# Half-width seven-product blocks in groups 1 to 3 of the last up projection of an fp32 SwiGLU layer

## The chip, the cores and the metric

The kernel runs on one core of a Trainium2 chip. The metric is device time in microseconds of one execution, the median of the runs shown. The core has a matrix engine (TensorE, PE in the profile, with its weight loads apart as PEld), VectorE (DVE), ScalarE (ACT), GpSimd (POOL) and SyncE (SP), which issues most of the DMA transfers. The engines run side by side, each through its own list of instructions in order; semaphores make one wait for another. TensorE takes one operand as weights, loaded beforehand, streams the other past them, and leaves its results in PSUM banks, from which ScalarE and VectorE read. All other on-chip data lie in SBUF.

## The reference

Attention over 8 batches of 12 heads with 448 tokens and 64 dimensions, with q and k normalised, and then a SwiGLU layer with 768 inputs and outputs and 1536 hidden columns over the 3584 tokens. All is fp32.

```python
q_n, k_n = rmsnorm(q, g_q), rmsnorm(k, g_k)
attn = softmax(q_n @ k_n.transpose(0, 1, 3, 2) / sqrt(64)) @ v
x = attn.transpose(0, 2, 1, 3).reshape(3584, 768)
g = x @ w_gate
val = x @ w_val
out = (g * sigmoid(g) * val) @ w_out
```

## The kernel before, in words

The function `fast` does everything for inputs of the usual size. Attention goes in pairs of heads. The layer goes in four blocks of two batches (`block`, n = 0 to 3), each with an **up** phase (gate and value products, silu, their product) and a **down** phase (output). Attention for the next block is laid into a block's time; the last block has none beside it.

The products are not plain matrix products. The input of a block is cut into 3 by 2 blocks, and the weights into 3 by 3, and a scheme with 15 instead of 18 block products is used: sums of weight blocks ("sides", made once and kept in DRAM as `up_sides` and `down_sides`) multiply sums of input blocks (`xs`, made per block), and each result is added into one or more of six sums. `UP_ORDER` is the order of the 15 products x, `UP_SUMS` the order in which the sides lie in DRAM, and `UP_READ` says into which sum (t0, t1, d, t3, t4, t5) a product goes, how, and which of six results k it completes. `FRESH` products open a PSUM bank, others add to one.

The up phase has four groups g of output columns. `up_product` (L1453) does one product for one group, once for gate (which = 0, PSUM tiles `mm`) and once for value (which = 1, tile `at`). Each is two matmuls of 128 by 128 weights with 448 tokens (L1474), a matmul of fp32 runs as two passes. One reader then takes the bank: ScalarE for a copy (L1409), VectorE for an addition or a subtraction (L1411, L1413, L1415). Gate sums lie in `gt`, value sums in `v0` to `v5`. When a result is complete, ScalarE's silu writes to a PSUM tile `st` (L1551) and VectorE multiplies it by the value sum into `gt` (`weigh`, L1554). `up_load` (L1569) brings the sides of five products at a time.

After a group, `combine` makes parts of the down phase's inputs: `hs` half 0 from results 0 and 1 (product 6, L1185) and half 1 from result 4 (product 1, L1189), for each group; product 10 then needs one long combine over all groups. `down_product` (L1663) does 15 products with four matmuls (one for each group) for two halves of the output, and begins with product 6, whose matmuls stream `hs` half 0, group by group.

The order of the instructions is not written by hand. `Order` (L365) collects pieces of work, each with an engine, a length, a due time `when`, a `rank` that brings it forward, and the pieces it must follow. `run` then places piece after piece on its engine as the planned times allow. Reads of PSUM banks have rank 60, silu and `weigh` rank 0, so reads come first.

Of the kernel before, what the change touches and what calls it, by code (L numbers as in the profile page):

```python
# [9 lines left out]
F32 = mybir.dt.float32  # L10
# [483 lines left out]
def fast(  # L494
# [73 lines left out]
        rr=4, ws=2, **{x + str(i): 1 for x in "vw" for i in range(6)},  # L568
# [14 lines left out]
    OFTEN = dict(w1=0, w2=1, w3=2, w4=3, rows=4)  # L583
# [52 lines left out]
    WS = 10 * NC2 * P  # L636
    up_sides = [dram.tile([P, 2, NC2, 15, P], F32, name=f"up_sides{g}") for g in range(NG)]
    down_sides = dram.tile([P, 2, NG, 15, P], F32, name="down_sides")

# [26 lines left out]
    UP, DOWN, BOTH = 30 * NG * PRODUCT, 90.7, 170.0  # L666
# [3 lines left out]

    def block_start(n):
        return FIRST + n * (UP + BOTH) + MORE * (n > 0)

    def block_end(n):
        return block_start(n) + UP + MORE * (n == 0)
# [722 lines left out]
    }  # L1398
    DOWN_READ = {
# [17 lines left out]
    def load_sides(key, sides, part, sums):  # L1417

        n = 2 * (NC2 if sums is UP_SUMS else NG)
        to = take(*key, [P, WS])[:, 0 : n * len(part) * P]  # L1420
# [18 lines left out]
    def block(n):  # L1439
        add = order.add  # L1440
        start = block_start(n)
        unit = (block_end(n) - start) / (30 * NG)
# [10 lines left out]
        def up_product(g, step, x, which, load, key):  # L1453
            nonlocal last
            when = start + (2 * (15 * g + step) + which) * unit

            b = ("BCDAE".index(CHAIN[x]) % 2 if CHAIN[x] != "E" else 0) ^ (g % 2) ^ (n > 0)
# [111 lines left out]
        def up_load(g, piece):  # L1569
            key = ("ws", (n, g, piece))  # L1570
            load = add(
                "SP", 1.2, start + (30 * g + 10 * piece) * unit - 24.0,
# [7 lines left out]

        for g in range(NG):
            steps = [(step, which) for step in range(15) for which in range(2)]
            if n == 0 and g == 0:
                steps[: 2 * HEAD] = sorted(steps[: 2 * HEAD], key=lambda of: of[::-1])
            for step, which in steps:
                if step % 5 == 0 and which == 0:
                    key, load = up_load(g, step // 5)
                up_product(g, step, UP_ORDER[step], which, load, key)
        up_done[n] = last
        if n < NB - 1:  # L1590
# [3 lines left out]
            )  # L1594
        bank_read[:] = [free[0, 0], free[0, 1]]
# [32 lines left out]
        for g in range(NG):  # L1628
            when = start + 30 * (g + 1) * unit + 1.0
# [3 lines left out]
        combine(10, h1, b1, None, block_end(n) + 3.0, [*all_hidden, *made[1], up_done[n]])  # L1633
# [5 lines left out]
        def down_product(step, x, s):  # L1639
# [3 lines left out]
            key = ("ws", (n, "o", piece))  # L1643
            size = 2 if piece < 7 else 1
            if piece not in loads:
# [3 lines left out]
                    after=[*last_load, *(weights["down", i] for i in range(2 * NG))], takes=[key],  # L1649
# [8 lines left out]
            def emit():  # L1658
# [3 lines left out]
                for g in range(NG):  # L1662
                    nc.tensor.matmul(  # L1663
                        banks[s][:, 0:S], w[:, s, g, at], where[x][:, g],
# [198 lines left out]
```

## Time and profile before

| what | before |
|---|---|
| time, median of 3 runs | 1455.13 us (1453.11 to 1456.28) |
| span of the profiled execution | 1452.0 us |
| last block, up phase, group 0 | 1174 to 1219 us |
| last block, up phase, groups 1 to 3 | 1219 to 1354 us |
| last block, down phase | 1354 to 1446 us |
| up phase of block 1 | about 473 to 654 us |

The profile shows one execution on the core, in microseconds from the start of the span. The span is what the profiler saw of that execution, from its first to its last instruction; the execution has no other time of its own on record beside the runs in the first row. In a row of the profile a group of instructions stands as line, engine, operation, tile written from tiles read, shapes and count, then the busy time and the mean of one in ns, then the idle time of the engine ahead of it and what ended that. A row of the timeline begins with start and length; on PE a row with x4 is four passes that follow one another, and its length includes the time until the last is out. In a row of windows each engine has its busy time and its count; then come the granted clock, the share of the DMA engines and GB/s.

### The profile page before, as it was taken

Reading aid. Unit: us, or ns where it says so; the run is one execution under the profiler, and the core shown is the slowest. Engines: PE = TensorE matmul, PEld = TensorE weight load, DVE = VectorE, ACT = ScalarE, POOL = GpSimd, SP = SyncE. Lnnn points to the kernel's source line nnn. Section 1 sums busy time; section 2 is a strip of 40 time slices with the busy share of each in tenths; the row PEclk is TensorE's granted clock in tenths of the full one; section 3 lists DMA queues with packets and bytes.
Section 4 is the critical chain, followed back from the end, with each engine's and each line's share of the span. In section 5 each row is a group of like instructions: output and inputs, shape, how many; then the busy total and the mean of one; then the engine's idle time right before and its main releaser. Section 6 shows DMA issues by size and latency. Waiting matters only on the chain.

```text
span 1452.0 us, 19362 instructions
## 1 busy us (share of the span) xinstructions
PE 1426.0 (98%) x6736; PEld 689.5 (47%) x6736; DVE 879.8 (61%) x1485; ACT 601.6 (41%) x1210; POOL 405.7 (28%) x476
## 2 busy tenths in 40 slices
PE   8999999999999999999999999999999999999997
PEld 4455454534444455544444455544444445555553
DVE  5889876878866434546877642455686644442533
ACT  6875444476653222356564122345555322212100
POOL 4756666625443000022443200011434300000000
PEclk9999999999999999999999999999999999999999
DMA  7778979854643533433644623443463452322235
GB/s 196 217 219 268 352 266 310 260 149 90 129 103 64 133 102 92 114 113 70 122 98 86 138 74 107 107 112 93 85 126 77 95 135 73 108 73 90 69 100 110
DMA packets 410416, 193.29 MB, mean 133 GB/s; under 512 B 280004, under 2 KB 390852, under 8 KB 410308
## 3 DMA queue, kind: packets, MB, share of 16 engines
q1 hardware_dynamic: 399040, 190.57, 49.1%
q10 hardware_dynamic: 11140, 1.38, 0.7%
q8 instruction: 55, 0.90, 0.3%
q14 instruction: 53, 0.43, 0.1%
q0 software_dynamic: 128, 0.00, 0.0%
HBM read 157.29 MB, written 34.60 MB: 132 GB/s over the span
## 4 chain that ended last, share of the span: by engine, by line
PE 90%; DMA 3%; DVE 2%; ACT 2%; SPq 1%; issue 1%; POOL 1%; ACTq 0%; DVEq 0%; POOLq 0%
PE at L1474 25%; PE mm L1474 25%; PE mm L1663 23%; PE at L1049 8%; PE st L970 7%; PE st L1080 1%; PE mm L1080 1%; DMA out_dram<-spare 1%; SPq L768 1%; DMA work<-in_k_dram 1%; ACT es L985 1%; DMA xs<-in_moe_w_gate_dram 0%; PE st L908 0%; DMA v<-in_v_dram 0%; ACT work L918 0%
## 5 line engine op out<-in xcount | busy, mean ns | idle before, releaser
L1474 PE MATMUL at<-xs,ws 128*128 128x448 f32 x960 | 401.2, 540 | 2.5 <-DVE v L1413 1.4
L1474 PE MATMUL mm<-xs,ws 128*128 128x448 f32 x960 | 401.7, 541 | 0.2 <-DVE hs L1315 0.2
L1474 PEld LDWEIGHTS at<-xs,ws 128*128 128x128 f32 x960 | 181.4, 190 | 184.7 <-issue 166.7
L1474 PEld LDWEIGHTS mm<-xs,ws 128*128 128x128 f32 x960 | 182.2, 190 | 180.7 <-issue 177.9
L888 POOL TENSOR_TENSOR work<-work,rr 128x448 f32<-128x448 f32 x72 | 71.8, 1016 | 467.5 <-DVE rr L715 341.6
L1663 PE MATMUL mm<-gt,ws 128*128 128x448 f32 x448 | 175.5, 543 | 0.0
L970 PE MATMUL st<-work 64*64 64x448 f32 (+1 forms) x1536 | 151.2, 501 | 10.3 <-ACT work L918 4.9
L985 ACT ACTIVATE es<-st 128x896 f32<-128x896 f32 x129 | 114.2, 914 | 101.6 <-PE at L1049 87.8
L1411 DVE TENSOR_TENSOR gt<-gt,mm 128x448 f32<-128x448 f32 x64 | 39.7, 621 | 188.1 <-PE mm L1474 161.7
L1663 PE MATMUL mm<-hs,ws 128*128 128x448 f32 x384 | 151.3, 544 | 0.0
L990 POOL TENSOR_TENSOR sums<-es 128x896 f32<-128x896 f32 x36 | 77.2, 2145 | 176.8 <-PE st L1080 83.7
L1663 PEld LDWEIGHTS mm<-gt,ws 128*128 128x128 f32 x448 | 83.6, 190 | 83.0 <-issue 80.8
L1551 ACT ACTIVATE st<-gt 128x448 f32<-128x448 f32 x96 | 52.3, 547 | 159.1 <-DVE gt L1415 85.7
L1409 ACT COPY gt<-mm 128x448 f32<-128x448 f32 x80 | 42.6, 532 | 157.5 <-PE mm L1474 157.4
L1049 PE MATMUL at<-es,v 64*64 64x448 f32 (+1 forms) x1032 | 106.0, 507 | 0.0
L1663 PEld LDWEIGHTS mm<-hs,ws 128*128 128x128 f32 x384 | 71.3, 190 | 71.0 <-issue 70.1
L970 PEld LDWEIGHTS st<-work 64*64 64x64 f32 x1536 | 50.9, 133 | 79.1 <-issue 37.4
L1409 ACT COPY v<-at 128x448 f32<-128x448 f32 x96 | 51.0, 532 | 80.4 <-PE at L1474 79.6
L990 POOL TENSOR_TENSOR sums<-sums,es 128x896 f32<-128x896 f32 x36 | 76.0, 2112 | 2.8
L1049 PEld LDWEIGHTS at<-es,v 64*64 64x64 f32 (+1 forms) x1032 | 44.1, 134 | 56.2 <-issue 50.4
L1554 DVE SCALAR_TENSOR_TENSOR gt<-st,v 128x448 f32<-128x448 f32 x96 | 59.7, 622 | 7.3 <-DVE v L1415 0.5
L1411 DVE TENSOR_TENSOR v<-v,at 128x448 f32<-128x448 f32 x64 | 39.8, 621 | 39.6 <-PE at L1474 39.5
(170 smaller groups left out, 1550.5 us busy)
## 6 DMA issues: line engine op xcount, KB each, us to landing
ws<-up_sides SPq DMA_DIRECT2D x32, 1024.0 KB, 5.6
ws<-down_sides SPq DMA_DIRECT2D x16, 1024.0 KB, 5.7
ws<-down_sides SPq DMA_DIRECT2D x28, 512.0 KB, 4.8
ws<-up_sides SPq DMA_DIRECT2D x16, 768.0 KB, 4.9
out_dram<-spare SPq DMA_DIRECT2D x168, 56.0 KB, 2.1
v<-in_v_dram SPq DMA_DIRECT2D x96, 96.0 KB, 2.5
ws<-up_sides SPq DMA_DIRECT2D x32, 256.0 KB, 5.9
ws<-up_sides SPq DMA_DIRECT2D x16, 512.0 KB, 5.8
```

Source lines behind the costliest of these rows:

```text
L888: nc.gpsimd.tensor_tensor(out=tiles["t", m][:, x], in0=tiles["qk", (m, x)], in1=rr.to_broadcast([P, NC, C]), op=ALU.mult,)
L970: nc.tensor.matmul(st[ds(D * x, D), h, 0:n], tiles["KT", m][rows, ds(P * j + D * of_keys, D)], tiles["QT", m][rows, ds(Q * of_queries, n)] ...
L985: nc.scalar.activation(e, tiles["st", (m, j)][:, :, 0 : S * width(j) // P], AF.Exp)
L990: nc.gpsimd.tensor_tensor(out=to, in0=tiles["e", (m, 0)] if j == 1 else to, in1=e, op=ALU.add)
L1049: nc.tensor.matmul(tiles["at", (m, x)][ds(D * h, D), ds(0, Q) if early else queries], tiles["v", m][rows, j, h], tiles["e", (m, j)][rows, ...
L1080: nc.tensor.matmul(to[ds(D * h + C * x, C)], halves[:, x] if half else many[:, 0:C], term[:, h, 0:Q] if half else term[:, h, ts(x, Q)], st ...
L1409: nc.scalar.copy(to, ps)
L1411: nc.vector.tensor_tensor(out=to, in0=old, in1=ps, op=ALU.add)
L1474: nc.tensor.matmul(ps(), w[:, which, c, at], xs[:, SLOT[x], c], start=fresh and c == 0, stop=c == NC2 - 1, skip_group_check=True,)
L1551: nc.scalar.activation(take(*act, [P, 2, TB])[:, 0, 0:S], to, AF.Silu)
L1554: nc.vector.scalar_tensor_tensor(to, tiles[act][:, 0, 0:S], 1.0 / SCALE, tiles[ready], op0=ALU.mult, op1=ALU.mult,)
L1663: nc.tensor.matmul(banks[s][:, 0:S], w[:, s, g, at], where[x][:, g], start=fresh and g == 0, stop=g == NG - 1, skip_group_check=True,)
```

## The change

In the last block, groups 1 to 3 (`SEVEN = {3: (1, 2, 3)}`) do each product x in another way. A product is two weight chunks (inputs) times gate and value (outputs) times two halves of 224 tokens, which is a 2 by 2 by 2 block product: eight half-width matmuls. A scheme of the Strassen-Winograd kind does it with seven, which are spread over four streams with PSUM banks of their own:

- X: A11 and S2 into an `mm` bank; Y: S1 and S3 into an `at` bank; Z: A12 and A22 into an `st` tile; W: S4 into half a bank of a second `st` tile. A11 to A22 are the chunk and token quarters of `xs`; S1 to S4 are sums and differences of them.
- Z and W run two products behind X and Y (`LAG`).
- Each stream is read and summed as the results were before, at 448 columns for X, Y and Z and 224 for W. When a result is complete in all four streams, POOL adds X's and Y's parts in four half-width additions (`plus`) and Z to the gate (`sow`, 448 wide), VectorE adds W's part to the value (`top`, 224 wide, both inputs in SBUF), ScalarE's silu goes from `gt` into free columns of the two W banks, and VectorE multiplies as before.
- Sums t5 and t0 have a second place for every second group (`sums`, `v`); the place of t4's Y sum is one.
- `halves_of` makes S1 to S4 for all 15 products on POOL during group 0 (60 subtractions and additions of 224 columns).
- The seven weight combinations are made ahead by `prepare`: 15 units for POOL (four subtractions of 384 columns each) with their loads and a store to DRAM (`up7`), 8 of them in the up phase of block 1 and 7 in that of block 2, planned 16 us apart. The last block loads three products at a time, X and Y apart from Z and W.
- `UP_SUMS` has another order (the sides' places in DRAM), the `ws` tiles are larger, and the first load of the last down phase goes to another buffer. In the last block, the combines of product 6 and 1 also wait for Y products of the last group that read from `hs` (`hs_free`), and the combine of product 10 for result 3 of all groups only.

The diff, cut to its core:

```diff
-    UP_SUMS = (8, 1, 7, 13, 10, 14, 3, 5, 11, 0, 4)
+    UP_SUMS = (8, 7, 1, 13, 10, 14, 3, 11, 4, 0, 5)
...
+    SEVEN = {3: (1, 2, 3)}
+    HALF, LAG = S // 2, 2
...
+    PREPARE, PREPARE_PACE, up7_done = {1: [(g, u) for g in (1, 2, 3) for u in range(5)][:8], 2: [(g, u) for g in (1, 2, 3) for u in range(5)][8:]}, 16.0, {}
...
+        def halves_of():
+            for step, x in enumerate(UP_ORDER):
...
+                for i, (to, one, two, op) in enumerate((
+                    ("S3", "A11", "A21", ALU.subtract), ("S2", "A22", "S3", ALU.subtract),
+                    ("S1", "S2", "A11", ALU.add), ("S4", "A12", "S2", ALU.subtract),
+                )):
+                    done = order.add(
+                        "POOL", 0.55, begin[seven[0] - 1] + (2 * step + 2) * unit + 0.6 * i,
...
+        PARTS = dict(
+            X=((0, "A11"), (3, "S2")), Y=((2, "S1"), (1, "S3")),
+            Z=((0, "A12"), (2, "A22")), W=((1, "S4"),),
+        )
...
+            for k in range(15 * len(seven) + LAG):
+                for stream in "XYZW":
+                    j = k - LAG * (stream in "ZW")
...
+                    for side, (slot, of) in enumerate(PARTS[stream]):
+                        nc.tensor.matmul(
+                            half(ps(), side), w[:, slot, at], part_of(of, x),
+                            start=fresh and side == 0, stop=True, skip_group_check=True,
+                        )
...
+                    if t == "t5" and j % 2:
+                        return spare_keys
+                    if t == "t0" and j % 2:
+                        return "v", (n, g, stream, t)
+                    X = {"t0": "v0", "t5": "v1", "t1": "v2", "t4": "v3", "t3": "v4", "d": "v5"}
+                    Y = {"t0": "w1", "t5": "w2", "t1": "w3", "t4": "w4", "t3": "rows", "d": "rows"}
...
+                if stream == "X":
+                    ready7["X"] = plus(Xr, Xr, Xl, when + 1.0, [done], [kx])
+                elif stream == "Y":
+                    u4 = plus(Yl, Xr, Yl, when + 1.0, [done, ready7["X"]], [kx, ky])
+                    u3 = plus(Xr, Xr, Yr, when + 1.7, [u4], [kx, ky])
+                    ready7[g, result] = u3, plus(Yr, Yl, Yr, when + 2.4, [u3], [ky])
...
+                        to = gt[:, g, result]
...
+                        eng.tensor_tensor(out=to, in0=to, in1=tile_at("X", t), op=ALU.add)
...
+                        to = half(tile_at("Y", t), 0)
+                        nc.vector.tensor_tensor(out=to, in0=to, in1=tile_at("W", t), op=ALU.add)
...
+                        return tiles[st_keys["W"]][:, :, TB // 2 : TB // 2 + HALF]
...
+                        nc.scalar.activation(room(), halves(gt[:, g, result]), AF.Silu)
...
+                    gated = order.add(
+                        "ACT", 0.55, when + 1.5, gate, after=[acc["gate", g, result], weighed], mode="silu",
...
+                when = start + 4.0 + j * PREPARE_PACE
...
+                for i, (to, one, two) in enumerate(((2, 1, 0), (3, 5, 2), (1, 5, 1), (6, 4, 3))):
...
+            if g in seven:
+                if g == seven[0]:
+                    sevens()
+                continue
...
-            combine(6, a1, a2, None, when, [hidden[g, 0], hidden[g, 1], *before], g)
-            combine(1, b2, h0, ALU.subtract, when, [made[6][g], hidden[g, 4], *before], g)
+            combine(6, a1, a2, None, when, [hidden[g, 0], hidden[g, 1], *before, hs_free[0]], g)
+            combine(1, b2, h0, ALU.subtract, when, [made[6][g], hidden[g, 4], *before, hs_free[1]], g)
```

How the planner places this is seen in the lists of instructions. Rows have the line in their own kernel, the operation, the tile written and those read, the columns, and the engines waited for. First, ScalarE at the border between groups 2 and 3 of the last block, in the kernel before: silus of the old group (`st` from `gt`), then copies of the new group's first gate and value products (`mm` and `at`).

```order
L1551 ACTIVATE st_8119<-gt_88 128x448 [waits DVE_49]
L1551 ACTIVATE st_8129<-gt_88 128x448 [waits DVE_49]
L1551 ACTIVATE st_8140<-gt_88 128x448 [waits DVE_49]
L1409 COPY gt_88<-mm1_93 128x448 [waits PE_49]
L1409 COPY v1_8152<-at_94 128x448 [waits DVE_49,PE_49]
L1409 COPY gt_88<-mm0_92 128x448 [waits PE_49]
L1409 COPY v0_8159<-at_94 128x448 [waits PE_49]
```

The same border on ScalarE after, where `mm` is X, `at` is Y, `st_8100` is Z, `st_8104` is W with the silu's columns, and `spare_81` holds the Y sums and some of W's.

```order
L1424 COPY v2_8560<-mm0_95 128x448 [waits PE_49]
L1424 COPY spare_81<-at_97 128x448 [waits PE_49]
L1424 COPY v3_8569<-mm1_96 128x448 [waits Pool_49]
L1424 COPY gt_91<-st_8100 128x448 [waits PE_49]
L1873 ACTIVATE st_8104<-gt_91 128x2x224 [waits DVE_49,PE_49]
L1424 COPY spare_81<-at_97 128x448 [waits DVE_49]
L1873 ACTIVATE st_8104<-gt_91 128x2x224 [waits Pool_49]
L1424 COPY spare_81<-st_8104 128x224 [waits DVE_49,Activation_49]
```

Silus now stand between the new group's copies, and the copy of a Y product (`spare_81<-at_97`) waits for VectorE. What it waits for is the last row here, on VectorE after: the fifth X product of the new group is read (L1426) ahead of the multiply of result 4 of the old one.

```order
L1876 SCALAR_TENSOR_TENSOR gt_91<-st_8104,v_8299 128x448 [waits DVE_49,Activation_49]
L1860 TENSOR_TENSOR spare_81<-spare_81,more_94 128x224
L1426 TENSOR_TENSOR v2_8560<-v2_8560,mm1_96 128x448 [waits PE_49,Activation_49]
L1876 SCALAR_TENSOR_TENSOR gt_91<-st_8104,spare_81 128x448 [waits DVE_49,Activation_49,Pool_49]
L1860 TENSOR_TENSOR spare_81<-spare_81 128x224
```

The second place is VectorE at the end of the up phase. Before, the combine into `hs` for group 3 (L1185, which the first down product waits for) stands amid the last reads.

```order
L1415 TENSOR_TENSOR gt<-mm_93,gt 128x448 [waits PE_49]
L1185 SCALAR_TENSOR_TENSOR hs<-gt 128x448 [waits DVE_49]
L1415 TENSOR_TENSOR v_8166<-at,v_8166 128x448 [waits PE_49]
L1554 SCALAR_TENSOR_TENSOR gt<-st,v_8166 128x448 [waits DVE_49,Activation_49]
L1415 TENSOR_TENSOR gt<-mm_92,w_8214 128x448 [waits PE_49]
L1189 TENSOR_TENSOR hs<-gt,hs 128x448 [waits DVE_49]
```

After, this combine (L1199) comes behind the last reads of Z and W (L1428) and five of the six results' additions and multiplies (L1860, L1876), of which the rows in the middle are left out.

```order
L1203 TENSOR_TENSOR hs<-gt,hs 128x448 x2
L1428 TENSOR_TENSOR spare<-spare,at 128x448 [waits PE_49]
L1430 TENSOR_TENSOR gt<-st,gt 128x448 [waits PE_49]
L1430 TENSOR_TENSOR more<-st,more 128x224 [waits PE_49]
...
L1428 TENSOR_TENSOR spare<-spare,st 128x224 [waits PE_49]
L1203 TENSOR_TENSOR hs<-gt,hs 128x448
L1860 TENSOR_TENSOR spare<-spare 128x224 [waits Pool_49]
L1876 SCALAR_TENSOR_TENSOR gt<-st,spare 128x448 [waits DVE_49,Pool_49]
...
L1860 TENSOR_TENSOR spare<-spare 128x224
L1199 SCALAR_TENSOR_TENSOR hs<-gt 128x448
L1876 SCALAR_TENSOR_TENSOR gt<-st,spare 128x448 [waits DVE_49,Activation_49]
```

On TensorE the rows of these products (L1474 before) become seven of 224 columns, in the order X, Y, Z, W. The new waits are those on ScalarE and VectorE, at the border between groups 2 and 3:

```order
L1737 MATMUL mm1_96<-xs_82,ws_8074 128x224 [waits Activation_49]
L1737 MATMUL mm1_96<-work_80,ws_8074 128x224
L1737 MATMUL at_97<-hs_92,ws_8074 128x224 [waits Activation_49]
L1737 MATMUL at_97<-xs_82,ws_8074 128x224
L1737 MATMUL st_8100<-xs_82,ws_8009 128x224 x2
L1737 MATMUL st_8104<-es_93,ws_8009 128x224 [waits DVE_49]
```

The matmul into `at_97` here waits for the copy of the Y product two before, and the one into `st_8104` for VectorE's reads of the W tile.

More of the change, by code (lines that the diff above doesn't have):

```diff
@@ L1419, in load_sides @@
         n = 2 * (NC2 if sums is UP_SUMS else NG)
-        to = take(*key, [P, WS])[:, 0 : n * len(part) * P]
+        if key[0] == "qk":
+            tiles[key] = work
+        else:
+            take(*key, [P, WS])
+        to = tiles[key][:, 0 : n * len(part) * P]
         to = to.rearrange("p (n x f) -> p n x f", n=n, f=P)
@@ L1441, in block @@
         start = block_start(n)
-        unit = (block_end(n) - start) / (30 * NG)
+        unit = PRODUCT + MORE * (n == 0) / (30 * NG)
+        begin = [start + (30 * g * unit if n == 0 else up_time(n, g)) for g in range(NG + 1)]
+        seven = SEVEN.get(n, ())
         last = down_done.get(n - 1)
@@ new lines, in restore @@
+        def restore():
+            for step, x in enumerate(UP_ORDER):
+                side_done.setdefault((n, x), []).append(
+                    order.add(
+                        "POOL", 0.55, third_done[x]["when"] + 1.0,
+                        lambda x=x: nc.gpsimd.tensor_tensor(
+                            out=part_of("A21", x), in0=part_of("A11", x), in1=part_of("S3", x),
+                            op=ALU.subtract,
+                        ),
+                        after=[third_done[x]], port=True,
+                    )
+                )
@@ L1588, in block @@
                 up_product(g, step, UP_ORDER[step], which, load, key)
+                old_done[UP_ORDER[step]] = last
+            if seven and g == seven[0] - 1:
+                halves_of()
+        if n in PREPARE:
+            prepare()
         up_done[n] = last
@@ L1642, in down_product @@
             piece = step // 2
-            key = ("ws", (n, "o", piece))
+            in_qk = n == NB - 1 and piece == 0 and NG - 1 in seven
+            key = ("qk" if in_qk else "ws", (n, "o", piece))
+            rest = [("qk", (n, "o", i)) for i in range(1, BUFS["qk"])] * in_qk
             size = 2 if piece < 7 else 1
@@ L1648, in down_product @@
                     lambda: load_sides(key, down_sides, DOWN_ORDER[2 * piece :][:2], DOWN_SUMS),
-                    after=[*last_load, *(weights["down", i] for i in range(2 * NG))], takes=[key],
+                    after=[*last_load, *(weights["down", i] for i in range(2 * NG))], takes=[key, *rest],
                     moves=[
@@ L1670, in down_product @@
                 after=[
-                    last, loads[piece], bank_read[s], *made.get(x, []),
+                    last, loads[piece], bank_read[s ^ turned_over], *made.get(x, []),
                     *(all_hidden if x in (14, 0, 5, 7) else []),
                 ],
-                uses=[key], mode="full",
+                uses=[key, *rest], mode="full",
             )
@@ L1687, in emit_read @@
                     old = tiles[value]
-                read(how, tiles[value], old, banks[s][:, 0:S])
+                read(how, tiles[value], old, banks[s ^ turned_over][:, 0:S])
             done = add(
```

283 lines of the change are left out of this document (270 added, 13 removed).

## The prediction

> **What bounds the kernel now.** I read the page first, for the engine that is busy all the time and for the chain that ended last.
>
> ```profile
> PE 1426.0 (98%) x6736; PEld 689.5 (47%) x6736; DVE 879.8 (61%) x1485; ACT 601.6 (41%) x1210; POOL 405.7 (28%) x476
> ...
> PEclk9999999999999999999999999999999999999999
> ...
> PE 90%; DMA 3%; DVE 2%; ACT 2%; SPq 1%; issue 1%; POOL 1%; ACTq 0%; DVEq 0%; POOLq 0%
> ```
>
> TensorE is busy for 98% of the span, at full clock, and is 90% of the chain. So time is won only by less work on TensorE, and lost wherever it is made to wait. The change touches the last block's up phase, so I cut that block into windows: the up phase's group 0, its groups 1 to 3, the down phase. Each row gives length, then busy time and count of PE, PEld, DVE, ACT and POOL.
>
> ```profile
> 1174.00:1219.50 45.50, 45.50 (x122) 23.00 (x122) 19.14 (x33) 10.95 (x19) 0.00 (x0) 1.00 0.34 97
> 1219.50:1354.00 134.50, 134.50 (x359) 67.98 (x358) 51.16 (x84) 28.89 (x54) 0.00 (x0) 1.00 0.27 86
> 1354.00:1446.00 92.00, 90.58 (x242) 45.45 (x240) 39.23 (x43) 6.51 (x13) 0.00 (x0) 1.00 0.44 102
> ```
>
> In groups 1 to 3 TensorE is busy 134.50 of 134.50 us; DVE has work for 38% of it, ScalarE for 21%, POOL for none. Every wait that the change brings there costs time at once, since none is there now.
>
> **The gain: fewer columns through TensorE.** Two rows of the timeline give the pace of a pass of 448 columns, and one in attention that of 224.
>
> ```profile
> 1179.84 1.67 PE L1474 MATMUL mm<-xs,ws 128*128 128x448 f32 x4
> 1181.34 1.67 PE L1474 MATMUL at<-xs,ws 128*128 128x448 f32 x4
> ...
> 116.56 1.68 PE L1049 MATMUL at<-gt,v 128*64 128x224 f32 x16
> ...
> L1049 PE MATMUL at<-gt,v 128*64 128x224 f32 x120 | 13.2, 358 | 0.0
> ```
>
> Four passes every 1.50 us are 0.376 us each. Of the 224-column ones two stand side by side (64 columns of weights each), so sixteen are eight pairs, and (1.68 − 0.358) / 7 = 0.189 us. That is half of 0.376 with nothing fixed on top. Before, a product takes 8 passes of 448: 45 products × 8 × 0.376 = 135.3 us. After, 7 matmuls of 2 passes of 224: 45 × 14 × 0.189 = 119.1 us. **Term A is −16.3 us** (−15 to −16.8: 0.187 is exactly half, 0.191 the slow end).
>
> It holds only if the weights are loaded in 0.189 us, unseen.
>
> ```profile
> L1474 PEld LDWEIGHTS mm<-xs,ws 128*128 128x128 f32 x960 | 182.2, 190 | 180.7 <-issue 177.9 <-DMA ws<-up_sides 0.9 <-DVE hs L1315 0.6
> ...
> 40.65 0.57 PE L908 MATMUL st<-ident,work 112*128 112x112 f32 x4 [0.20 <-ACT more L985]
> ...
> L908 PE MATMUL st<-ident,work 112*128 112x112 f32 x96 | 12.0, 265 | 2.1 <-POOL work L881 1.1 <-ACT es L985 0.8 <-ACT more L985 0.2
> ```
>
> A load of 128 columns is booked with 0.190 us, but that is half of the pass beside it. The transposes load 128 columns each and follow one another in (0.57 − 0.265) / 3 = 0.10 us, so a load fits. [...]
>
> **Term B: the borders between groups.** Four streams of results now share ScalarE and DVE. These rows price the steps.
>
> ```profile
> 1175.33 1.67 PE L1474 MATMUL at<-xs,ws 128*128 128x448 f32 x4
> 1175.53 0.53 ACT L1409 COPY gt<-mm 128x448 f32<-128x448 f32 x1 [5.51 <-PE mm L1474]
> ...
> L1411 DVE TENSOR_TENSOR v<-v,at 128x448 f32<-128x448 f32 x64 | 39.8, 621 | 39.6 <-PE at L1474 39.5
> L1409 ACT COPY v<-at 128x448 f32<-128x448 f32 x96 | 51.0, 532 | 80.4 <-PE at L1474 79.6 <-DVE gt L1554 0.7
> L1554 DVE SCALAR_TENSOR_TENSOR gt<-st,v 128x448 f32<-128x448 f32 x96 | 59.7, 622 | 7.3 <-DVE v L1415 0.5
> L1551 ACT ACTIVATE st<-gt 128x448 f32<-128x448 f32 x96 | 52.3, 547 | 159.1 <-DVE gt L1415 85.7 <-DVE gt L1413 33.1 <-DVE gt L1528 23.5
> L985 ACT ACTIVATE es<-st 128x896 f32<-128x896 f32 x129 | 114.2, 914 | 101.6 <-PE at L1049 87.8 <-PE st L970 13.3
> ```
>
> A reader starts 0.20 us after TensorE leaves a bank (1175.33 to 1175.53). At a border DVE first reads the fifth X product (0.62), then multiplies result 4 of the old group (0.62), and only then may ScalarE copy the third Y product (0.53) into the one place that result 4's Y sum has just left. Two products later TensorE wants that Y bank. From the end of X4's matmuls the bank comes free after 0.20 + 0.62 + 0.62 + 0.53 = 1.97 us, and with no slack left TensorE stands about **2.0 us**. Queued behind that copy on ScalarE are a silu and the two copies of S4 products, which open the next W matmuls. Silu now writes into the S4 stream's own banks, so the next W matmul also waits for the silu and the multiply of the result before. One that comes due while they run waits up to 0.547 + 0.622 and two hand-overs of 0.03 (below), 1.23 us; I take half, 0.62, three times at a border. So 2.0 + 3 × 0.62 = 3.86 us, at two inner borders: **+7.7 us**. The bounds: nothing waits but the one copy (2 × 2.0 = 4), or each W matmul waits in full (2 × (2.0 + 3 × 1.23) = 11). The middle is nearest to these rows, since no order ties a W matmul's place to the moment at which a silu begins.
>
> **Terms C and D: the end of the third group.** The tail before, the costly combine, and POOL's durations:
>
> ```profile
> 1347.45 0.62 DVE L1185 SCALAR_TENSOR_TENSOR hs<-gt 128x448 f32<-128x448 f32 x1
> ...
> 1352.92 0.62 DVE L1413 TENSOR_TENSOR gt<-gt,mm 128x448 f32<-128x448 f32 x1
> ...
> 1353.57 0.55 ACT L1551 ACTIVATE st<-gt 128x448 f32<-128x448 f32 x1 [2.46 <-DVE gt L1413]
> ...
> 1354.22 4.30 PE L1663 MATMUL mm<-hs,ws 128*128 128x448 f32 x11
> ...
> L1189 DVE TENSOR_TENSOR hs<-gt 128x1792 f32<-128x1792 f32 x8 | 16.2, 2025 | 2.9 <-PE mm L1663 2.7
> ...
> L1336 POOL TENSOR_TENSOR work<-work 128x128 f32<-128x128 f32 x20 | 8.6, 456 | 0.3
> ...
> L1336 POOL TENSOR_TENSOR work<-work 128x256 f32<-128x256 f32 x4 | 2.9, 728 | 0.0
> ...
> L990 POOL TENSOR_TENSOR sums<-es 128x896 f32<-128x896 f32 x36 | 77.2, 2145 | 176.8 <-PE st L1080 83.7 <-ACT es L985 63.9 <-ACT xs L1142 29.2
> ```
>
> A silu begins 0.03 us after DVE's end (1353.54 to 1353.57). Straight lines give estimates for the new widths: from 621 ns for 448 columns and 2025 for 1792, 0.39 us for 224 on DVE; from 532 for 448 and 914 for 896, 0.34 on ScalarE; from 456 ns for 128 and 728 for 256, POOL takes 0.66 us for 224, 1.0 for 384 and 1.14 for 448 (the row of 896, 2.145 us, is on that line).
>
> C: a read of Z, the last but two, stands on DVE behind two combines into hs (0.62 each), which take both inputs from SBUF while POOL's additions run: 2 × 0.62 and about 1 us of blocking (below), **+2.2 us** (1 to 3).
>
> D: before, the combine for group 3 was done at 1347.45, and the down phase began at 1354.22 with no stop. After, it is the last but three on DVE, behind everything that the late streams close. Counted from the last W matmul: hand-over 0.20, W's read 0.39, a combine 0.62, six half additions 6 × 0.39 = 2.3, five multiplies 5 × 0.62 = 3.1, the combine 0.62: 7.3 us. Each multiply also waits for a silu that waits for the multiply before: 0.55 + 2 × 0.03 − 0.39 = 0.22 more, four times 0.9. The down phase starts with groups 0 to 2, three ready matmuls of 2 × 0.376 = 2.25 us. So 7.3 + 0.9 − 2.25 = 5.9 us. The half additions take both inputs from SBUF while POOL adds too, and these two rows show what that does:
>
> ```profile
> 301.88 2.34 POOL L990 TENSOR_TENSOR sums<-es 128x896 f32<-128x896 f32 x1 [3.72 <-ACT es L985]
> 302.14 2.56 DVE L1528 TENSOR_TENSOR gt<-gt,w 128x448 f32<-128x448 f32 x1
> ```
>
> An addition of 0.62 us lasted 2.56, until POOL's was over. Two or three such meetings with POOL's 0.66 to 1.14 us are 2 us: **D = +7.9 us** (5 with no meeting and a shorter queue, 10 with twice as many). [...]
>
> **Term E: preparation, and what is hidden.** Group 0 gets 60 POOL additions of 224 columns: 60 × 0.66 = 39.6 us in 45.1, where POOL does nothing now (x0). They need no other engine, so 0; without that cover the first S1 product would wait for the rest. Blocks 1 and 2 get 15 preparations of up to four loads, four POOL subtractions of 384 columns (60 × 1.0 us in all) and a store.
>
> ```profile
> 482.00:650.00 168.00, 168.00 (x472) 83.93 (x471) 69.15 (x124) 55.54 (x109) 7.37 (x8) 1.00 0.39 106
> ...
> ws<-up_sides SPq DMA_DIRECT2D x16, 768.0 KB, 4.9
> ```
>
> In block 1's up phase POOL is busy 7.37 of 168 us and the DMA engines 39%, so 8 preparations of about 2.1 MB (100 GB/s more) fit. A store waits on SP for POOL, and behind it on SP stand the loads of sides and of attention, which are issued some 24 and 10 us ahead. What remains: attention's scores move one or two products forward at the end of both blocks, two places in each where they may come before ScalarE has freed their bank. Such a wait lies between nothing and one of ScalarE's 0.914 us; ScalarE is busy a third of the time there (55.54 of 168), so I take a third, 0.3: **+1.2 us** (0 to 3.7). The last block's own loads come for three products at a time, 4 × 3 × 64 KB = 768 KB for X and Y, and 576 KB for Z and W; 768 KB land in 4.9 us, three products take 3 × 2.65 = 7.9, and there are three and two places: 0. The first Z and W products may each wait for one read of 0.62 us more than now: **+0.8** (0 to 1.2).
>
> **Sum.** −16.3 + 7.7 + 2.2 + 7.9 + 1.2 + 0.8 = **+3.5 us**. The down phase loses nothing else. The profiled execution has a span of 1452.0 us, the median of the runs is 1455.13, and I let the 3.1 us between them stay: 1452.0 + 3.5 + 3.1 = 1458.6, to the half microsecond **1458.5 us**. 0.2% is about what a measurement of this kernel can tell from no change, 2.9 us: 1452.2 to 1458.0 is the same.
>
> **Rivals.**
> - **The closing work is less in the way (same, 1455.5).** The half additions meet no addition of POOL, so D is 5.9 (−2.0), and one of the three waits of W at each border falls away (−1.2): +0.3, 1455.4. For it: in a group DVE's own work is 27 reads of 0.62, 9 of 0.39, 4 additions for 2.3, 6 half additions of 0.39, 6 multiplies of 0.62 and 2 combines, 30 of 39.8 us. Against: the work comes in a burst at the border, where spare time elsewhere doesn't help.
> - **It pays (faster, 1448.5).** Place: the borders. If result 4's multiply is done before X4's matmuls end, the copy of the third Y product waits for nothing. It decides when that multiply lies 2.0 us earlier than I count; then B is 2, C 1 and D 5.5, the small waits 0: −16.3 + 2 + 1 + 5.5 + 1.2 = −6.6. For it: ScalarE has only 28.89 us of work in 134.50 now, and DVE 51.16. Against: the multiply is queued behind X4's read on DVE, in a fixed order.
> - **The closing work is the bound (slower, 1469.5).** POOL needs 6 × (4 × 0.66 + 1.14) = 22.7 us in a group, but five results close in a row: 5 × 3.8 = 19 us against 5 × 2.65 = 13.3. If the 5.7 us come through at all three bursts, that is 17; about 6 of it lie in B's waits already, so 11 more. It decides when a burst starts with less than 5.7 us of room. Against: between bursts POOL catches up, and Z and W run two products late.
> - **The loads don't fit (slower, 1578).** 0.19 more for each of 630 passes, 120 us. The transposes speak against it.
>
> **Chances.** Forecast 0.45 (1455.5 to 1462, a sixth of it under 1458.0), the closing work less in the way 0.25, it pays 0.16, the closing work as the bound 0.12, the loads 0.02. So slower 0.52, the same 0.32, faster 0.16. The range 1449 to 1467 leaves out half of "it pays", most of the bound and the loads, some 0.18; one of B, C and D can go to its bound within it.
>
> **What would show it.** In the profile after: the 224-column passes of the last block 0.189 us apart (A); at each inner border a gap of 2 us ahead of a Y product, ended by a ScalarE copy, and short ones ahead of W products (B); one gap of some 8 us after the third matmul of the down phase, ended by DVE's combine (D), with half additions of over 1 us beside POOL's (the meetings); blocks 0 to 2 unchanged to 1 to 2 us (E). A border without gaps, a tail gap under 6 us, or passes at another pace would make the prediction wrong.

## The result, and the profile after

| | median us | lowest to highest | ratio to before, 95% interval |
|---|---|---|---|
| before | 1454.86 | 1453.11 to 1456.28 | |
| after | 1466.83 | 1465.14 to 1467.51 | 1.0083, 1.0068 to 1.0097 |

The change costs 12.0 us. The time is 8.3 us over the number given and lies inside the forecast range by 0.2 us only; two of the four runs (1467.04 and 1467.51) lie above the range. In number the result is nearer to the rival in which the closing work is the bound (1469.5) than to the forecast (1458.5). The span of the profiled execution grows from 1452.0 to 1463.4 us, and these 11.4 us are what the traces can be asked about.

First the page after, its engines and the chain, and then windows of the last block: groups 1 to 3 and the down phase (columns as before: length, then busy time and count of PE, PEld, DVE, ACT, POOL, the granted clock, the share of the DMA engines, GB/s).

```profile
PE 1416.9 (97%) x7006; PEld 738.5 (50%) x7006; DVE 919.0 (63%) x1563; ACT 613.2 (42%) x1244; POOL 573.4 (39%) x686
...
PE 86%; DMA 4%; DVE 4%; ACT 2%; SPq 2%; issue 2%; POOL 1%; ACTq 0%; DVEq 0%; POOLq 0%
```

```profile
1222.00:1354.90 132.90, 124.20 (x632) 117.48 (x631) 80.74 (x150) 40.09 (x86) 66.49 (x89) 1.00 0.46 156
1354.90:1454.00 99.10, 91.32 (x238) 45.86 (x237) 46.85 (x56) 9.12 (x17) 5.57 (x6) 0.97 0.36 82
```

TensorE has 9 us less to do in the span, and its share of the chain falls from 90% to 86%: it now stands. Groups 1 to 3 take 132.9 us where they took 135.3 (1218.9 to 1354.2), so 2.4 are won, not 16. The down phase, 97.8 us from its first matmul to the end of the span before (1354.2 to 1452.0), takes 108.5 (1354.9 to 1463.4): 10.7 lost. The last block begins at 1176.9 in place of 1173.8: 3.1 lost ahead of it.

The view of waits names what TensorE stood for. Its columns are the waiting tile and line, the releaser, the total in us, how often, and the longest.

```profile
PE mm L2037 <- DVE hs L1199: 7.8, 1, 7.8
...
PE at L1737 <- ACT spare L1424: 3.8, 2, 1.9
...
PE st L1737 <- DVE gt L1876: 2.1, 4, 0.6
PE st L1737 <- DVE gt L1430: 1.9, 1, 1.9
...
PE st L1737 <- ACT st L1873: 0.9, 2, 0.5
```

Each of the four waits that the prediction priced is there: the first is the down phase's wait for the combine, the second the Y copy at two borders, the third and fifth the W products behind silu and multiply, the fourth the end of the third group. One border, from the timeline:

```profile
1272.29 0.58 ACT L1873 ACTIVATE st<-gt 128x448 f32<-128x448 f32 x1
...
1273.17 0.62 DVE L1426 TENSOR_TENSOR v<-v,mm 128x448 f32<-128x448 f32 x1 [4.13 <-PE mm L1737]
1273.71 0.61 DVE L1876 SCALAR_TENSOR_TENSOR gt<-st,spare 128x448 f32<-128x448 f32 x1
...
1274.36 0.53 ACT L1424 COPY spare<-at 128x448 f32<-128x448 f32 x1 [1.48 <-DVE gt L1876]
...
1274.94 0.65 PE L1737 MATMUL at<-hs,work 128*128 128x224 f32 x2 [1.88 <-ACT spare L1424]
```

The silu of the old result ends at 1272.87 (1272.29 + 0.58). Its multiply begins 0.84 us later, at 1273.71, since the read of the fifth X product stands ahead of it on DVE, which had been idle for 4.13 us until then. The copy then waits for the multiply, and TensorE for the copy. So the order on DVE makes up 0.84 of the 2.04 us; the silu itself was no earlier.

### The profile page after: what moved, and what is told of

It is laid out like the page before. It is cut to its first block, busy times and chain, and to the rows that moved or that the text cites. A ratio compares the mean times of both kernels' runs of the same rounds, so it can differ in the third digit from the quotient of the medians.

```text
span 1463.4 us, 20469 instructions
## 1 busy us (share of the span) xinstructions
PE 1416.9 (97%) x7006; PEld 738.5 (50%) x7006; DVE 919.0 (63%) x1563; ACT 613.2 (42%) x1244; POOL 573.4 (39%) x686
## 4 chain that ended last, share of the span: by engine, by line
PE 86%; DMA 4%; DVE 4%; ACT 2%; SPq 2%; issue 2%; POOL 1%; ACTq 0%; DVEq 0%; POOLq 0%
PE mm L2037 22%; PE at L1495 20%; PE mm L1495 19%; PE at L1063 7%; PE st L984 7%; PE st L1737 3%; PE at L1737 2%; PE mm L1737 2%; DMA work<-in_k_dram 1%; SPq L782 1%; PE st L1094 1%; PE mm L1094 1%; DMA out_dram<-spare 1%; ACT es L999 1%; DMA v<-in_v_dram 1%
## 5 line engine op out<-in xcount | busy, mean ns | idle before, releaser
L1495 PE MATMUL at<-xs,ws 128*128 128x448 f32 x780 | 326.3, 541 | 4.7 <-DVE v L1428 3.6
L1495 PE MATMUL mm<-xs,ws 128*128 128x448 f32 x780 | 325.2, 540 | 0.2 <-DVE hs L1329 0.2
L1495 PEld LDWEIGHTS at<-xs,ws 128*128 128x128 f32 x780 | 147.1, 190 | 153.6 <-issue 134.8
L1495 PEld LDWEIGHTS mm<-xs,ws 128*128 128x128 f32 x780 | 147.9, 190 | 146.2 <-issue 144.5
L2037 PE MATMUL mm<-hs,ws 128*128 128x448 f32 x352 | 139.2, 545 | 0.0
L1426 DVE TENSOR_TENSOR gt<-gt,mm 128x448 f32<-128x448 f32 x52 | 32.2, 620 | 142.3 <-PE mm L1495 140.5
L1063 PE MATMUL at<-es,v 64*64 64x448 f32 (+1 forms) x1032 | 106.2, 508 | 0.0
L1572 ACT ACTIVATE st<-gt 128x448 f32<-128x448 f32 x78 | 42.6, 547 | 125.9 <-DVE gt L1430 69.9
L1424 ACT COPY gt<-mm 128x448 f32<-128x448 f32 x65 | 34.6, 532 | 126.0 <-PE mm L1495 125.9
L1928 POOL TENSOR_TENSOR es<-es 128x384 f32<-128x384 f32 x32 | 31.2, 997 | 121.4 <-DMA es<-up_sides 120.7
L1424 ACT COPY v<-at 128x448 f32<-128x448 f32 x79 | 41.9, 531 | 63.6 <-PE at L1495 62.5
L936 DVE STREAM_TRANSPOSE work<-work 128x448 f32<-128x448 f32 x72 | 45.5, 637 | 24.9 <-POOL work L902 21.0
```

The lines of the kernel that those rows point to most:

```text
L936: nc.vector.transpose(to, tiles["t", m][:, x].rearrange("p c f -> p (c f)"))
L1063: nc.tensor.matmul(tiles["at", (m, x)][ds(D * h, D), ds(0, Q) if early else queries], tiles["v", m][rows, j, h], tiles["e", (m, j)][rows, ...
L1424: nc.scalar.copy(to, ps)
L1426: nc.vector.tensor_tensor(out=to, in0=old, in1=ps, op=ALU.add)
L1495: nc.tensor.matmul(ps(), w[:, which, c, at], xs[:, SLOT[x], c], start=fresh and c == 0, stop=c == NC2 - 1, skip_group_check=True,)
L1572: nc.scalar.activation(take(*act, [P, 2, TB])[:, 0, 0:S], to, AF.Silu)
```

## The experiments

Each changes the kernel after (or, where said, a kernel of this list). The kernel before ran on the same chip beside each set; ratios are to those runs. Spans and starts of blocks are from each run's profiled execution.

**Only the preparation.** The last block is computed as before.

```diff
-    SEVEN = {3: (1, 2, 3)}
+    SEVEN = {}
...
-        for g in sorted({g for gs in SEVEN.values() for g in gs})
+        for g in (1, 2, 3)
```

> The changed kernel, but with the last block computed as before: the weight combinations are still made and stored in blocks 1 and 2 and are used by nothing. Theory (the work ahead of the last block costs what the trace shows, its up phase begins 3.1 us later in the span): 1455 + 3 = about 1458 us, with the last block's up phase beginning some 3 us later than before. Rival (those 3 us are scatter between two executions, the cost lies in the last block alone): 1455 us, within 1 us of the kernel before.

Measured: 1457.52 us, ratio 1.0009 (0.9999 to 1.0019), between the two and not clear of no change. Blocks 1 and 2, from the first up product of one block to that of the next, last 348.2 and 347.7 us; they lasted 347.3 and 346.9 before, and 348.2 and 347.5 in the kernel after. So the preparation costs some 1.5 us, and the other 1.6 that the kernel after was late lie ahead of block 1, where nothing was added; they count as scatter. That the new units have no part in it is not shown: the first up product of block 1 comes between 479.3 and 486.5 us in the nine profiled executions with 15 units, and between 479.1 and 480.4 in the four with ten or none. The last block, from its first up product to the end of the span, takes 278.2 us here, as before; in the kernel after it takes 286.4. In this run too something lies ahead of block 1: TensorE's clock is at half in one more stretch of block 0.

```profile
309.20:312.60 3.40, 3.40 (x6) 1.11 (x4) 1.95 (x4) 2.77 (x4) 0.00 (x0) 0.51 0.27 45
```

**The stop at the end, filled.** Ten matmuls run into a bank that nobody reads, ahead of the one that waits.

```diff
                 for g in range(NG):
+                    if n == NB - 1 and step + s == 0 and g == NG - 1:
+                        for _ in range(10):
+                            nc.tensor.matmul(
+                                at_banks[:, 0, 0:S], w[:, s, 0, at], where[x][:, 0],
+                                start=True, stop=True, skip_group_check=True,
+                            )
```

> The changed kernel with ten idle-time matmuls of 448 columns (0.75 us each) into an unused PSUM bank, ahead of the matmul that waits 7.8 us at the start of the last down phase. Theory (TensorE's clock is granted at half after its long stop, and six passes then take 0.747 us in place of 0.376): the passes after the stop are 0.376 us apart and the time falls by 2.2 us, to 1464.6. Rival (the half pace comes from the operands or the combine beside it, not from the stop): passes still 0.747 us apart, 1466.8 us.

Two windows of the kernel after, ahead of and behind the end of the half clock, and one of this run at the same place in the program:

```profile
1365.07:1369.40 4.33, 4.33 (x6) 2.18 (x7) 3.03 (x3) 0.53 (x1) 0.00 (x0) 0.50 0.00 0
1369.40:1373.73 4.33, 4.33 (x13) 2.11 (x12) 2.02 (x1) 0.53 (x1) 0.00 (x0) 1.00 0.00 0
```

```profile
1370.87:1374.00 3.13, 3.13 (x9) 1.64 (x10) 3.03 (x3) 0.53 (x1) 0.00 (x0) 1.00 0.03 5
...
PE mm L2043 <- DVE hs L1199: 0.3, 1, 0.3
```

After the stop of 7.8 us six passes took what thirteen take later (the counts take in passes that lie across an edge; the passes are 0.747 us apart, later 0.376). With the stop filled there are nine passes in 3.13 us, at full clock. The time was 1465.07 us, ratio 1.0059 (1.0039 to 1.0080): less than after by about what the half clock costs, though the intervals overlap. The traces show it more clearly: from the first matmul of the down phase to the end of the span it is 106.2 us, 2.3 less than the 108.5 of the kernel after. The profiled execution is the slowest of the five runs, at 1468.6 us. Its last block begins 4.8 us later than that of the kernel after (1181.8 and 1176.9), and groups 1 to 3 take 1.0 us more, with half clock behind the stop at the first border here.

```profile
1279.90:1283.30 3.40, 3.40 (x9) 2.72 (x10) 1.16 (x2) 1.10 (x4) 0.00 (x0) 0.50 0.00 0
```

**A second place for the fourth Y sum**, in columns of `work` that are free in this block.

```diff
+                    if stream == "Y" and t == "t4" and j % 2:
+                        return held[-1]
...
+                    if stream == "Y" and t == "t4" and j % 2:
+                        return work[:, 5408:5856]
```

> The changed kernel with a second place for the fourth Y sum in the middle group, so that the copy of the third Y product waits for no multiply at both inner borders. Theory (this wait is 2.04 us at each border): both gaps go, 1466.8 - 4.3 = 1462.5 us. Rival (the engines' queues are the limit, the wait only moves to the next Y or W product): the gaps shrink by less than a half, 1465 to 1467 us.

```profile
PE mm L2041 <- DVE hs L1199: 7.8, 1, 7.8
PE st L1737 <- ACT st L1877: 7.4, 4, 3.3
PE st L1737 <- DVE gt L1430: 1.9, 1, 1.9
...
```

The Y copy waits no more, but at both borders a W product now waits up to 3.3 us for silu (L1877), and half clock follows (3.4 us each, at 1279.9 and 1327.7). 1468.09 us, ratio 1.0079 (1.0052 to 1.0106). The mechanism of the rival held, its time did not: the wait moved, and grew.

**Seven products in two groups**, 1 and 2; group 3 is as before, and 10 units are prepared, five in each block.

```diff
-    SEVEN = {3: (1, 2, 3)}
+    SEVEN = {3: (1, 2)}
```

> Seven products in groups 1 and 2 alone, group 3 as before. Theory (the loss at the end is the burst of closing work ahead of the down phase; before a group of full-width products it is hidden): 30 products save 10.8 us, one border of 4.7, start waits of 1.5, the entry into group 3 about 2, blocks 0 to 2 about 2: 1455 us, no stop of over 3 us and no half clock. Rival (the burst stops the first full-width products of group 3 as it stops the down phase): a stop of 5 us or more there, 1460 us or over.

```profile
PE at L1737 <- ACT spare L1424: 2.3, 2, 1.9
PE st L1737 <- ACT st L1873: 2.1, 2, 1.8
PE st L1737 <- DVE gt L1430: 1.2, 1, 1.2
PE st L1737 <- DVE gt L1876: 0.5, 1, 0.5
```

1454.70 us, ratio 0.9996 (0.9984 to 1.0007): no change from before, 12 us below three groups. The wait for the combine is gone, since group 3's wide products run beside the closing work. The number of the theory (1455) was met, but partly by luck: blocks 0 to 2 cost nothing, where the theory had 2 us (the last block begins at 1173.1, before at 1173.8), and the last block takes 279.2 us, 1.0 more than before, where the theory's terms give 2.6 less. A half clock of 6.8 us (1272.0 to 1278.9), which the theory had ruled out, is part of it. Blocks 1 and 2 last 347.3 and 346.5 us, no longer than before, with 10 units.

**Silu out of the W banks**, in place in `gt`, alone and with the second place.

```diff
-                        nc.scalar.activation(room(), halves(gt[:, g, result]), AF.Silu)
+                        nc.scalar.activation(gt[:, g, result], gt[:, g, result], AF.Silu)
...
-                            halves(gt[:, g, result]), room(), 1.0 / SCALE, halves(tile_at("Y", t)),
+                            gt[:, g, result], gt[:, g, result], 1.0 / SCALE, tile_at("Y", t),
...
-                        "ACT", 0.55, when + 1.5, gate, after=[acc["gate", g, result], weighed], mode="silu",
+                        "ACT", 0.55, when + 1.5, gate, after=[acc["gate", g, result]], mode="silu",
```

> The changed kernel with the silu in place in gt (SBUF), out of the W banks; the multiply then reads two SBUF inputs. Theory (a W product waits because silu and multiply hold its banks, 0.55 to 0.72 us at six places): these gaps go, the 2.04 us gaps stay, 1466.8 - 3.5 = 1463.3 us. Rival (the multiplies now lock against POOL and are later by as much): 1466 us or more.

> The silu out of the W banks and the second place for the fourth Y sum together. Theory (the two waits cover each other: with either left, TensorE stands at a border, as the second place alone showed): no gap over 1 us at the borders, 1466.8 - 8 = 1459 us. Rival (the queues of ScalarE and DVE are the limit, not the places): a gap of over 1.5 us stays at each border, 1463 us or more.

Alone, first the waits and then one multiply of the timeline:

```profile
PE mm L2036 <- DVE hs L1199: 8.8, 1, 8.8
PE at L1737 <- ACT spare L1424: 3.8, 2, 1.9
PE st L1737 <- ACT spare L1424: 2.2, 2, 1.1
...
```

```profile
1261.97 1.44 DVE L1876 SCALAR_TENSOR_TENSOR gt<-gt,spare 128x448 f32<-128x448 f32 x1
```

With the second place as well:

```profile
PE mm L2040 <- DVE hs L1199: 8.8, 1, 8.8
PE st L1737 <- ACT spare L1424: 5.0, 2, 2.5
...
```

1468.98 us (1.0097, 1.0069 to 1.0124) and 1465.97 us (1.0057, 1.0031 to 1.0083). Both rivals held. W products no longer wait for silu, but for the copy that takes the W product before: the half addition of the last result frees its place (the run with a place for it, below, bears this out). Multiplies that read two SBUF inputs beside POOL take up to 1.44 us, and the stop at the end is 1 us longer.

**Two groups with both mends**, and then with a second place for the W sums t5 and t0 too, in free columns of the `qk` buffers.

```diff
+                    if stream == "W" and t in ("t5", "t0") and j % 2:
+                        return qk_keys[-1]
...
+                    if stream == "W" and t in ("t5", "t0") and j % 2:
+                        return half(work[:, 1536:1984], t == "t0")
```

> Seven products in groups 1 and 2 alone, with the silu out of the W banks and the second place. Theory: against the run with two groups the border gaps of 2.05, 2.15 and 0.65 us and the half clock that followed them go, about -6.5: 1448.5 us, faster than before. Rival (the closing work then stops group 3's first products instead): 1453 to 1455 us.

> The run with two groups, silu in SBUF and the second Y place, with a second place for the W sums t5 and t0 as well. Theory (the 2.85 us gap left at its border is the W copy that waits for the last half addition of the old group, which frees that place): this gap falls under 0.7 us, 1450.4 - 2.3 = 1448 us, the lowest of all. Rival (again only the next place is late): a gap of 2 us or more stays, 1450 us or more.

Waits of the first, and of the second:

```profile
PE st L1737 <- ACT spare L1424: 2.7, 1, 2.7
PE st L1737 <- DVE gt L1430: 1.2, 1, 1.2
...
```

```profile
PE st L1737 <- DVE gt L1430: 1.2, 1, 1.2
PE mm L1737 <- ACT v L1424: 0.9, 1, 0.9
PE at L1737 <- ACT spare L1424: 0.4, 1, 0.4
```

1450.36 us, ratio 0.9969 (0.9950 to 0.9989), and 1447.74 us, ratio 0.9965 (0.9953 to 0.9977). The first missed its number by 2 us, because of the 2.7 us wait for the W copy; with a place for that too the wait is gone. The second is the fastest kernel of the study, 0.35% under before. The ratios of the two do not tell them apart, as they were set against different runs of before; the missing wait does, and so does the length of the last block in the traces: 278.2 us before, 274.4 in the first and 271.9 in the second.

**The end of three groups, reordered.** The combine of product 6 for group 3 comes as soon as its results are multiplied, the combines of product 1 behind it.

```diff
-            combine(6, a1, a2, None, when, [hidden[g, 0], hidden[g, 1], *before, hs_free[0]], g)
-            combine(1, b2, h0, ALU.subtract, when, [made[6][g], hidden[g, 4], *before, hs_free[1]], g)
+            early = 8.0 * (bool(seven) and g == NG - 1)
+            combine(6, a1, a2, None, when - early, [hidden[g, 0], hidden[g, 1], *before, hs_free[0]], g)
...
+        for g in range(NG if seven else 0):
+            combine(1, b2, h0, ALU.subtract, when, [made[6][NG - 1], hidden[g, 4], *before, hs_free[1]], g)
```

> The changed kernel with the combine for product 6 of group 3 set as soon as its two results are multiplied, and the combines for product 1 behind it. Theory (the stop at the start of the down phase is the DVE queue ahead of that combine): the 2.05 us gap at the end of the group goes, the stop falls from 7.9 to about 4.5 us and its half clock goes or halves, 1466.8 - 2 - 3.4 - 2 = 1459.5 us. Rival (POOL's additions release the results so late that the combine comes no earlier): a stop of over 7 us, 1465 us or more.

```profile
PE mm L2041 <- DVE hs L1199: 3.9, 1, 3.9
PE at L1737 <- ACT spare L1424: 3.8, 2, 1.9
...
PE mm L2041 <- DVE hs L1203: 1.5, 1, 1.5
...
PE st L1737 <- DVE gt L1430: 0.7, 2, 0.3
```

1462.93 us, ratio 1.0056 (1.0037 to 1.0076). The gap at the end of the group falls from 1.9 to 0.7 (two of 0.3), the stop from 7.8 to 3.9, and the half clock behind it from 6.8 to 3.4 us (1361.6 to 1365.0). Of the gain 1.5 go back to the second down product, whose combine (L1203) is now late. In this execution a half clock of 3.4 us also follows the stop at the first border, which costs groups 1 to 3 about 1.0 us; the kernel after had none there.

**Three groups, all mends**: silu in SBUF, both second places, the end reordered, ten filling matmuls; then seven, with the last silus ahead of the down phase's first copies.

```diff
-                        "ACT", 0.55, when + 1.5, gate, after=[acc["gate", g, result]], mode="silu",
+                        "ACT", 0.55, when + 1.5, gate, after=[acc["gate", g, result]], mode="silu", rank=60.0 * (j == len(seven) - 1),
...
-                after=[last, drained.get((s, t))],
+                after=[last, drained.get((s, t)), *(gates if seven and step == 0 else [])],
```

> Seven products in three groups with all mends together: silu in SBUF, second places for the fourth Y sum and for the W sums t5 and t0, the combine set early, ten matmuls that fill the stop. Theory (each loss has its own cause, and they add): against the changed kernel 1466.8 - 7.5 (borders) - 2 (end of group 3) - 3 (stop) - 2.2 (half clock) = 1452 us, about 3 us over the two groups. Rival (with three groups DVE and POOL are the limit whatever the places): 1458 us or more.

> The run with three groups and all mends, with seven filling matmuls in place of ten, and the last silus ahead of the first two copies of the down phase on ScalarE (they stood behind them, and the multiplies and combines of the second down product waited for that). Theory (the 12 us that the run with all mends missed lie in its fill, 2.1 us too long, in the 2.3 us stop of the second down product and the half clock that followed, 1.9): 1458.7 - 6 = 1452.5 us. Rival (the closing work of three groups on DVE and POOL ends no earlier whatever its order): the down phase's second product still waits over 2 us, 1456 us or more.

The first gave 1458.71 us (1.0040, 1.0025 to 1.0056), 6.7 over its number. Groups 1 to 3 then took 124.8 us, 8.1 less than after, so the borders were mended. The loss was at the end, in part in the ten filling matmuls (the combine is done at 1355.2, the matmul that waits for it begins at 1357.3), the rest in ScalarE's queue:

```profile
1358.26 0.53 ACT L1424 COPY v<-mm 128x448 f32<-128x448 f32 x1 [7.08 <-PE mm L2054]
1358.69 0.58 ACT L1881 ACTIVATE gt<-gt 128x448 f32<-128x448 f32 x1
1361.26 0.53 ACT L1424 COPY w<-mm 128x448 f32<-128x448 f32 x1 [2.00 <-PE mm L2054]
1361.69 0.58 ACT L1881 ACTIVATE gt<-gt 128x448 f32<-128x448 f32 x1
```

A silu stood behind the copy of a down product, which waited for TensorE; the multiplies and the second product's combines waited for that silu, and TensorE for them (2.3 us at 1363.6, with a half clock from 1364.6 to 1368.0). With the order turned and three filling matmuls fewer, the waits of TensorE over 0.2 us in the last block are these, and the time is 1452.20 us, ratio 0.9983 (0.9974 to 0.9993), as expected within 0.3 us:

```profile
PE mm L1737 <- ACT v L1424: 1.9, 2, 0.9
PE st L1737 <- DVE gt L1430: 0.7, 2, 0.3
```

So three groups can be faster than before too. They remain over two groups, 0.9983 against 0.9965; the intervals just touch, but the last block takes 273.7 us here and 271.9 in the fastest kernel, and the preparation has 15 units and not ten. The seven filling matmuls alone are 14 passes of 0.376, 5.3 us, that TensorE spends on nothing. The two edits of the last run were not tried apart.

## Why the prediction was right, and where it was short

| term | predicted us | in the traces |
|---|---|---|
| A, fewer columns | −16.3 | −16.2: 45 products in 119.1 us of passes |
| B, two inner borders | +7.7 | +9.5 |
| C, end of the third group | +2.2 | +2.15 |
| small waits of the new streams | +0.8 | +2.1 |
| D, stop before the down phase | +7.9 | +7.9 |
| half clock after that stop | none | +2.25 |
| E, preparation | +1.2 | +1.5 |
| ahead of block 1, and after the last product | none | +2.1, taken as scatter |
| sum | +3.5 | +11.3 (spans: +11.4) |

**The direction and the mechanisms were right, the size was not.** Of the 11.3 us the sum had 3.5; that the range still held the time is luck as much as reckoning, since its upper bound, 1467, was meant for one of B, C and D at its bound, and not for a half clock and three terms that are each too small. Passes of 224 columns follow one another in 0.189 us, with their weight loads unseen. Each border has its gap of 2.04 us ahead of a Y product (2.0 predicted), ended by the copy named, and three shorter ones of 0.55 to 0.72 ahead of W products (0.62 predicted). The stop at the end is 7.94 us with the combine of group 3 at its end; reordering that queue halved it. This match is not luck: the six half additions ahead of the combine take 4.24 us in all (1.31, 1.20, 0.59 and three of 0.38), where the prediction had 2.3 and 2 for meetings with POOL.

The half additions met POOL as expected:

```profile
1355.95 1.51 POOL L1850 TENSOR_TENSOR gt<-gt,v 128x448 f32<-128x448 f32 x1
...
1356.40 1.31 DVE L1860 TENSOR_TENSOR spare<-spare 128x224 f32<-128x224 f32 x1
...
1358.19 2.36 POOL L1850 TENSOR_TENSOR gt<-gt,v 128x448 f32<-128x448 f32 x2
1358.36 1.20 DVE L1860 TENSOR_TENSOR spare<-spare,more 128x224 f32<-128x224 f32 x1
```

A half addition needs 0.38 us where POOL rests. The multiplies, one input in PSUM, kept their length (622 ns before, 621 after); with silu in SBUF, in the fastest kernel, they did not (814). Their groups, after and in the fastest kernel:

```profile
L1876 DVE SCALAR_TENSOR_TENSOR gt<-st,spare 128x448 f32<-128x448 f32 x16 | 9.9, 621 | 2.2 <-ACT st L1873 1.2 <-DVE spare L1860 0.5
```

```profile
L1884 DVE SCALAR_TENSOR_TENSOR gt<-gt,spare 128x448 f32<-128x448 f32 x9 | 7.3, 814 | 0.8 <-DVE spare L1868 0.5
```

**The step that failed is "The down phase loses nothing else."** A stop of 7.8 us costs more than itself: TensorE's clock is then granted at 0.50 until 1369.4, and the passes until then take 2.25 us more (0.16 of it is a late second pass, 0.908 us behind the first; the next follow in 0.747). The trace of before could have said so; there, too, the clock is at half in block 0. The prediction read "at full clock" off a row with 40 slices of 36 us each, in which 3.4 us at half clock still leave a 9.

```profile
296.40:299.80 3.40, 3.40 (x12) 1.23 (x15) 1.23 (x3) 0.81 (x1) 1.75 (x2) 0.50 0.81 165
```

Half-clock stretches in these runs lasted 3.4 us (above), 6.8 (1362.6 to 1369.4 after) and, with silu alone moved, 10.2 (1360.3 to 1370.5). TensorE was not always idle ahead of them: in the 3.41 us ahead of the stretch above (293.02 to 296.43) it was busy for 1.24 us, in those ahead of the 6.8 (1359.18 to 1362.59) it was idle.

**B and the small waits were mis-sized**, 9.5 for 7.7 and 2.1 for 0.8. Part of it is a cost of stops that the sum lacked: at seventeen places in the three groups the pass behind the first one after a stop comes 0.293 us later, not 0.189, so each adds 0.10, together 1.8 us. Three Y products at the start also come 0.1 to 0.2 us late each, presumably for S1 (the trace names POOL for the first of them alone). **E** was right in size; that the scores' move makes it was not tried, and with 10 units it vanishes. The 3.1 us by which the last block begins late are more than the "1 to 2 us" that the prediction allowed; half of them stay without a cause.

**The rivals.** "It pays" named the border as its place, and a single mend there doesn't bring it: the second place alone moved the wait to W (1468.09). That the closing work is the bound (1469.5) came nearest in time, and was half right: it sets the end of three groups, where nothing wide runs beside it, but in two groups it is covered.

## What to carry to other kernels

When a full engine's work is cut by a new scheme, the gain goes first to the queues that empty its results: price the last steps before a phase that needs all results, and put them beside wide work of the old kind, as two groups of three did here. Where one place or bank holds an engine up, list who else waits at that point before freeing it. Here a second Y place and the silu outside the banks brought 1 us or nothing when tried alone or together in three groups; with two groups they brought 4 us, and a second W place 2.5 more. And a stop of some microseconds is priced with the half clock that may follow it: 2.25 us behind the stop of 7.94 here.

## What the runs showed of the hardware

- A stop of 2.04 us at the border had no half clock behind it in the kernel after, but 3.4 us of it at the same place in the runs with the filled stop (1279.9 to 1283.3) and with the end reordered (1276.3 to 1279.7). Up to there the code is the same. The half clock costs groups 1 to 3 about 1.0 us.
- In the traces of before and after, half-clock stretches begin and end whole steps of 3.413 us apart: before, the beginnings at 296.43 and 1446.72 by 337 steps; after, the beginning at 1362.60 and the end at 1369.42 by 2, and that end and the beginning at 1458.17 by 26. Here are the 3.41 us ahead of the half clock in the run with the filled stop, and after the step with the most of the same stop, whose edge cuts the stop:

```profile
1276.52:1279.93 3.41, 1.53 (x8) 0.91 (x7) 1.76 (x4) 1.93 (x5) 0.00 (x0) 1.00 0.04 14
```

```profile
1273.87:1277.28 3.41, 1.78 (x8) 1.43 (x8) 2.21 (x5) 2.10 (x5) 0.00 (x0) 1.00 0.00 0
```

  So the same stop had half clock behind it in one execution, with 1.53 us of work on TensorE in the step, and none in another, with 1.78. The work in the step alone does not tell which: the kernel after has steps with less than the first, 1.46 us (304.46 to 307.88) and 1.52 (1355.77 to 1359.18), and full clock behind them. Where the stop falls on the steps may decide it; no run was made to test that.
- At seventeen stops in the three groups the second pass of a half-width matmul comes 0.10 us late (0.293 us behind the first, against 0.189). In the stop shown above, which ends at 1274.94, the weight loads of both passes take from 1274.94 to 1275.24, and the second pass begins at 1275.24. That it waits for its load was not tried.
